# Inverting 16x16 instead of 32x32 blocks on VectorE in the first four rounds, with one more doubling on TensorE

## The chip, the cores and the metric

One core of one Trainium2 chip. The metric is the device time of one execution in microseconds (us). Engines: PE is TensorE, PEld its weight load, DVE is VectorE, ACT is ScalarE, POOL is GpSimd, SP is SyncE, which here only issues transfers (its queue is written SPq). In the timelines below VectorE, ScalarE and SyncE work through their instructions in the order in which the program gave them: what stands first in such a queue and waits holds up all that stands behind it (10.89 us at VectorE's `x`, in the profile after).

## The reference, cut to what matters

```python
for t in range(S):                                  # S = 768 steps, batch 4, 8 heads of width 40
    y[:, :, t] = einsum('bhd,bhde->bhe', rt, state)
    Sa = einsum('bhde,bhe->bhd', state, at)
    state = state * wt[:, :, None, :] - einsum('bhd,bhe->bhde', Sa, bt) + einsum('bhd,bhe->bhde', vt, kt)
x = y.transpose(0, 2, 1, 3).reshape(3072, 320)
h = x @ w_in                                        # 320 -> 1024
e = exp(h - max(h)); solu = h * e / (sum(e) + 1e-9)
ln = (solu - mean) / sqrt(var + 1e-6) * g_ln
return ln @ w_out                                   # 1024 -> 320
```

The kernel does the recurrence in 12 rounds of 64 steps. Within a round the term with `Sa` couples each step to the earlier ones; that is a triangular system, so every round needs the inverse of a unit triangular 64x64 matrix per batch and head.

## The kernel before

A round is two iterations of the main loop (even: batches 0 and 1, odd: 2 and 3), 24 in all. The parts that the argument touches, with cuts marked by `...`:

```python
def gather(n):                      # 64 blocks of 32x32, from DRAM, where scatter put them
    nb = of_round[n]["nb"] = two.tile([P, Q, Q], FP32, tag="blk", name="blk", bufs=2)
    for p in range(2):
        nc.sync.dma_start(out=nb[half(p)], in_=of_round[n]["blocks"])

def invert(n):                      # 30 steps, two VectorE operations each
    ...
    for j in range(1, Q - 1):
        ...
        nc.vector.tensor_tensor(out=t, in0=nb[...], in1=u[...], op=ALU.mult)
        nc.vector.tensor_tensor(out=u[...], in0=u[...], in1=t, op=ALU.subtract)
        yield
    nc.vector.tensor_copy(out=ut, in_=u.rearrange("p c t -> p t c"))
    ...                             # stores u and ut to DRAM; bring_inverse fetches them

def solve(i):                       # one doubling: from 32x32 inverses to a 64x64 inverse
    for q, t in zip((0, 2), products("py", [left(0), left(2)])):
        nc.scalar.copy(out=y_mid[quarter(q + 1)], in_=t)
    yield
    for q, z in zip((0, 2), products("pz", [right(0), right(2)])):
        nc.scalar.mul(out=tinvT[quarter(q), :, :, quarter(1)], in_=z, mul=-1.0)
    yield

def readout(i):
    ...
    if s == 0:                      # one buffer: waits until the last round's repack has read it
        of_round[n]["x"] = two.tile([P, G, 2, P], FP32, tag="x", name="x", bufs=1)
    nc.vector.tensor_tensor(out=of_round[n]["x"][...], in0=t[...], in1=d["exT"][...], op=ALU.mult)

def repack(n):                      # x to xT, the layout that the MoE part reads: 12 transfers
    ...
EARLY = ("r r a W I r f W r r I W y r W a f L a I W s a f W a f I W s I f a W f", ...)
for i in range(N):
    ...                             # MoE work starts in iteration 6
    turns(EARLY[len(js) - 1] if i < LAG else STEADY, dict(I=inverse_steps(i)), **parts)
```

`turns` tells one step of each part per letter, and that is the order in every engine's queue: `r` recurrence, `y` readout, `I` inverse steps of the next round (as many as `inverse_steps` says at each place), `s` solve for the next iteration, `a`, `f`, `g` the products that prepare later iterations, `L` loads, `W` narrowing of the MoE weights from 64-bit floats (fetch on SP, arithmetic on DVE and ACT).

## Time and profile before

| | before |
|---|---|
| time, median of 3 runs at first | 722.13 us |
| first `pu` (end of the start-up) | 64.0 us |
| iterations 0 to 6, from `pu` to `pu` | 25.3, 29.2, 26.4, 25.1, 27.3, 25.1, 25.8 us |
| later iterations while the MoE part runs beside them | 24.3 us (24.30 and 24.38 in turn) |
| PE, DVE, ACT, POOL busy | 84, 65, 38, 11% |

`pu` is the product that applies the finished inverse, once an iteration. I took its start from TensorE's timeline, so a list of iteration lengths is one profiled execution each, good to about 1 us. First, TensorE's longest waits in iterations 1 to 5 of the kernel before (columns: who waits and for whom, then us in total, number of times, longest):

```profile
PE pbT L267 <- ACT tinvT L505: 18.7, 5, 5.9
PE pcx L347 <- ACT y_mid L502: 9.9, 5, 5.3
```

Then VectorE's waits in the same stretch. VectorE waits twice, in the even iterations 2 and 4, for the transfers that still read `x`, and three times, in the odd ones, for the gathered blocks:

```profile
DVE x L602 <- DMA xT<-x: 11.6, 2, 6.7
DVE u L410 <- DMA blk<-blk_dram: 9.9, 3, 4.7
```

### The profile page before, as it was taken

The numbers are of one execution on the slowest core, as the hardware profiler recorded it, in microseconds if no ns is written. First come the engines' busy times: TensorE is split into PE (matmuls) and PEld (weight loads), VectorE is DVE, ScalarE is ACT, GpSimd is POOL, SyncE is SP. The second block draws the span as 40 slices with busy tenths as digits, with TensorE's granted clock in tenths as the row PEclk, the third lists the DMA queues.
The fourth block names the chain that finished last, engine by engine and source line by source line (L and its number), as shares of the span: only waits on it lengthen the run. The fifth ranks groups of instructions, "written<-read, shape, count | busy, mean of one in ns | idle before, by whom it ended". The sixth has DMA issues, their size and how long they took to land.

```text
span 719.9 us, 25430 instructions
## 1 busy us (share of the span) xinstructions
PE 606.7 (84%) x10873; PEld 428.9 (60%) x10873; DVE 468.7 (65%) x1310; ACT 275.1 (38%) x654; POOL 77.7 (11%) x128
## 2 busy tenths in 40 slices
PE   4524866767658899999999999999999899979997
PEld 3423655556546666667766666666666666545554
DVE  2387969658656959687687596786876754232442
ACT  3322534343343534443454345344533344312322
POOL 3202010010010111011100110111000000000000
PEclk9856975786797999999999999999999999998999
DMA  9964553743765353545554626545325131000001
GB/s 175 163 114 81 122 108 77 142 97 72 141 108 93 67 99 70 110 85 91 100 96 90 105 57 108 102 88 103 65 49 103 27 64 33 21 23 18 19 7 30
DMA packets 269791, 59.82 MB, mean 83 GB/s; under 512 B 255464, under 2 KB 265328, under 8 KB 269680
## 3 DMA queue, kind: packets, MB, share of 16 engines
q1 hardware_dynamic: 266416, 57.48, 42.8%
q8 instruction: 86, 1.41, 0.9%
q10 hardware_dynamic: 3264, 0.72, 0.7%
q14 instruction: 25, 0.20, 0.1%
HBM read 40.08 MB, written 13.37 MB: 74 GB/s over the span
## 4 chain that ended last, share of the span: by engine, by line
PE 54%; DVE 21%; DMA 8%; ACT 7%; issue 5%; SPq 5%; ACTq 0%; DVEq 0%
PE po L668 15%; PE h L623 10%; DVE u L422 6%; DVE prod L420 5%; PE pyo L595 4%; PE plnT L663 4%; PE pcx L347 3%; PE pcum L334 2%; DVE nmax L633 2%; DMA ut_dram<-ut 2%; PE ppsi L286 2%; DMA blk<-blk_dram 2%; PE plamu L286 2%; PE pyo L517 2%; PE plamv L286 2%
## 5 line engine op out<-in xcount | busy, mean ns | idle before, releaser
L623 PE MATMUL h<-w_in,xT 128*128 128x512 f32 (+1 forms) x288 | 128.2, 635 | 3.9 <-DVE e L640 3.9
L668 PE MATMUL po<-w,lnT 128*128 128x320 f32 x384 | 114.8, 438 | 0.0
L422 DVE TENSOR_TENSOR u<-u,prod 128x30 f32<-128x30 f32 (+4 forms) x360 | 96.5, 268 | 12.3
L420 DVE TENSOR_TENSOR prod<-blk,u 128x30 f32<-128x30 f32 (+4 forms) x360 | 93.5, 260 | 11.5 <-DMA blk<-blk_dram 1.0
L668 PEld LDWEIGHTS po<-w,lnT 128*128 128x128 f32 x384 | 69.0, 190 | 26.2 <-issue 2.9
L337 POOL TENSOR_TENSOR kx<-raw_b,inv 128x320 f32<-128x320 f32 x24 | 21.0, 877 | 351.3 <-ACT inv L335 308.0
L633 DVE TENSOR_REDUCE nmax<-h 128x1 f32<-128x1024 f32 x24 | 29.3, 1221 | 44.9 <-PE h L623 44.9
L623 PEld LDWEIGHTS h<-w_in,xT 128*128 128x128 f32 (+1 forms) x288 | 38.2, 191 | 31.7 <-issue 29.8
L602 DVE TENSOR_TENSOR x<-pyo,kx 128x512 f32<-128x512 f32 x24 | 16.6, 692 | 60.8 <-PE pyo L595 49.1
L673 ACT ACTIVATE osb<-po,rs 128x320 f32<-128x320 f32 x24 | 12.7, 527 | 96.9 <-PE po L668 76.3
L347 PE MATMUL pcx<-cst,lw 128*128 128x132 f32 x192 | 34.3, 311 | 10.3 <-ACT y_mid L502 9.9
L347 PEld LDWEIGHTS pcx<-cst,lw 128*128 128x128 f32 x192 | 29.8, 214 | 19.4 <-ACT y_mid L502 15.2
L664 ACT COPY lnT<-plnT 128x512 f32<-128x512 f32 x48 | 28.0, 594 | 33.2 <-PE plnT L663 33.2
L637 ACT ACTIVATE e<-h,nmax 128x1024 f32<-128x1024 f32 x24 | 26.7, 1114 | 36.2 <-DVE nmax L633 36.2
L267 PE MATMUL pbT<-cst,kx 128*128 128x128 f32 x96 | 17.9, 321 | 25.8 <-ACT tinvT L505 18.7
L640 DVE TENSOR_TENSOR e<-h,e 128x1024 f32<-128x1024 f32 x24 | 29.4, 1225 | 14.8 <-ACT e L637 14.3
L334 PE MATMUL pcum<-lw,cst 128*128 128x320 f32 x48 | 23.2, 572 | 18.4 <-ACT lw L330 9.0
L663 PE MATMUL plnT<-cst,e 128*128 128x128 f32 x192 | 31.4, 294 | 6.2 <-DVE e L640 5.4
L288 DVE TENSOR_TENSOR lamv<-plamv,cst 128x512 f32<-128x512 f32 x24 | 16.5, 689 | 27.3 <-PE plamv L286 27.2
L505 ACT ACTIVATE tinvT<-pz 32x256 f32<-32x256 f32 x48 | 17.8, 372 | 42.5 <-PE pz L490 42.0
L267 PEld LDWEIGHTS pbT<-cst,kx 128*128 128x128 f32 x96 | 12.3, 163 | 35.4 <-issue 35.4
L663 PEld LDWEIGHTS plnT<-cst,e 128*128 128x128 f32 x192 | 22.1, 147 | 18.3 <-ACT kT L269 6.6
(104 smaller groups left out, 1087.8 us busy)
## 6 DMA issues: line engine op xcount, KB each, us to landing
blk<-blk_dram SPq DMA_DIRECT2D x24, 256.0 KB
raw_k<-in_k_dram SPq DMA_DIRECT2D x24, 160.0 KB
v<-in_v_dram SPq DMA_DIRECT2D x24, 160.0 KB
r<-in_r_dram SPq DMA_DIRECT2D x24, 160.0 KB
out_dram<-osb SPq DMA_DIRECT2D x24, 160.0 KB
raw_w<-in_w_dram SPq DMA_DIRECT2D x23, 160.0 KB
raw_b<-in_b_dram SPq DMA_DIRECT2D x23, 160.0 KB
raw_a<-in_a_dram SPq DMA_DIRECT2D x23, 160.0 KB
```

Source lines behind the costliest of these rows:

```text
L267: nc.tensor.transpose(out=t[:, g * P:(g + 1) * P], in_=pair(src, g), identity=ident)
L286: nc.tensor.matmul(t[half(c ^ p * cross), p, g * L:(g + 1) * L], lhsT=lhs[half(p), g, half(c)], rhs=rhs[half(p), g, half(c)], start=True, ...
L334: nc.tensor.matmul(t[:, 0:DM], lhsT=c_("cum_in"), rhs=lw[:, :, 0:D], start=True, stop=True)
L347: nc.tensor.matmul(t[:, g * 132:g * 132 + 132], lhsT=pair(lw, 2 * j + g), rhs=cst[:, lo:lo + 132], start=True, stop=True)
L420: nc.vector.tensor_tensor(out=t, in0=nb[:, j:j + 1, j + 1:Q].to_broadcast([P, rows, m]), in1=u[:, 0:rows, j:j + 1].to_broadcast([P, rows, ...
L422: nc.vector.tensor_tensor(out=u[:, 0:rows, j + 1:Q], in0=u[:, 0:rows, j + 1:Q], in1=t, op=ALU.subtract)
L595: nc.tensor.matmul(t[half(p), c, g * W:g * W + used], lhsT=kb[half(c), j, 2 * g + p, :], rhs=lam[half(c), h % 2, h // 2, 0:used], start=i ...
L623: nc.tensor.matmul(h[:, j * 512:j * 512 + 512], lhsT=of_round[i // 2]["xT"][rows, kt, i % 2 * P:i % 2 * P + P], rhs=w_in[rows, 4 if kt == ...
L633: nc.vector.tensor_reduce(out=nmax, in_=h, axis=AX.X, op=ALU.max, negate=True)
L640: nc.vector.tensor_tensor(out=q, in0=h, in1=e, op=ALU.mult)
L663: nc.tensor.transpose(out=t[:, j * P:(j + 1) * P], in_=q[:, f * P:(f + 1) * P], identity=ident)
L668: nc.tensor.matmul(o[:, 0:DM], lhsT=lnT[:, f, :], rhs=w2[:, f, :], start=f == 0, stop=f == NF - 1)
```

## The change

The intent: VectorE's inversion is on the path of the start-up and of the early iterations, so give it half the rows (28 short operations instead of 60) in rounds 0 to 3 and let TensorE, which waits there, do the doubling from 16 to 32 by products. Two copies go from ACT to POOL, the first loads are reordered, and six products whose result nobody reads are put ahead of the first chains. The diff, cut to its core (`...` marks cuts):

```diff
+FINE = 4
...
-        nc.scalar.copy(out=keyed(a)[:, :, :, 0:D], in_=by_heads(given(i, "a")))
+        nc.gpsimd.tensor_copy(out=keyed(a)[:, :, :, 0:D], in_=by_heads(given(i, "a")))
...
+    def invert_fine(n):
+        ...
+        for j in range(1, R - 1):                       # R = 16
+            ...                                         # the same two VectorE operations
+        for key, t, src in (("ut", ut, x.rearrange("b c t -> b t c")), ("u", u, x)):
+            for z in range(2):
+                nc.scalar.copy(out=t[half(z)][:, :, R * z:R * z + R], in_=src[half(z)])
+            for z in range(2):
+                nc.sync.dma_start(out=dst[:, R * z:R * z + R, :], in_=t[half(z)])
...
-        nc.scalar.copy(out=lamv[:, :, :, L:], in_=...)
+        nc.gpsimd.tensor_copy(out=lamv[:, :, :, L:], in_=...)
...                                                      # in solve:
+        if fine:
+            t = products("py16", [... for q in range(4)])
+            nc.scalar.copy(out=y_mid, in_=t[:, 0])
+            yield
+            t = products("pz16", [... for q in range(4)], [... for q in (0, 2)])
+            for q in (0, 2):
+                nc.vector.scalar_tensor_tensor(out=x, in0=t[quarter(q), 1, :, :, 0:R], scalar=c_("low")[quarter(q)],
+                                               in1=x, op0=ALU.mult, op1=ALU.add)
+            for q in range(4):
+                nc.scalar.mul(out=tinvT[rows, :, :, c:c + R], in_=t[rows, 0, :, :, R:Q], mul=-1.0)
+            yield
...
-    EARLY = ("r r a W I r f W r r I W y r W a f L a I W s a f W a f I W s I f a W f", ...
+    EARLY = ("r r a W I r f W r r I W y r W a s f L a W I s W a f a W s I f a W s I f W f", ...
...                                                      # inverse_steps, iterations 1 to 4
-            return [0, 0, 6, 6, 5 if i < LAG - 1 else 2] if i % 2 else [4, 4, 4, 3, 0]
+            return [0, 0, 2, 3, 3] if i % 2 else [3, 3, 2, 0, 0]
...                                                      # before the loop
-        load(0, "k", "v")
+        load(0, "k")
+        warm(3, sm_t[0].rearrange("q c g d -> q (c g d)"))
...                                                      # v and r later, weights behind round 0's gather
+        warm(3, of_round[0]["spilt"])
```

In what follows "sums" are the two VectorE operations after `pz16` and "scalings" the four ScalarE ones.

## The prediction

> **What bounds the kernel now.** I read four views in this order: the page's busy totals and slices, a table of four stretches, the chain of waits inside one early round, and TensorE's own waits in the late part. One round is two iterations of the main loop (0 to 23), one inversion and one block of each input. Iteration i is told by its `pu` product. The timeline has `pu` at 63.99, 89.32, 118.47, 144.84, 169.94, 197.23 and 222.32 us (iterations 0 to 6) and about every 24.4 us after that.
>
> ```profile
> PE   4524866767658899999999999999999899979997
> PEclk9856975786797999999999999999999999998999
> 0.00:64.00 64.00, 27.75 (x378) 22.08 (x378) 33.65 (x115) 18.40 (x43) 10.36 (x23) 0.75 0.84 141
> 64.00:222.30 158.30, 108.52 (x2483) 88.68 (x2482) 115.05 (x377) 65.18 (x173) 16.54 (x24) 0.78 0.54 105
> 222.30:640.00 417.70, 399.47 (x7769) 278.19 (x7770) 290.06 (x763) 171.81 (x404) 47.00 (x74) 0.99 0.42 78
> ```
>
> The columns of the last three lines are PE, PEld, DVE, ACT, POOL, then granted clock, DMA share and GB/s. From 222 us on PE is busy 96% of the time at clock 0.99: there PE is the bound. Before that it is busy 43% and 69% at clock 0.75 and 0.78, and DVE is the busiest engine (73% in the second stretch). So the kernel has three parts: a start-up of 64 us, six early iterations of 158 us (26.4 each), and a part limited by PE. The change can win only where PE waits.
>
> The start-up is one series of waits; the chain's lines around round 0's inversion:
>
> ```profile
> 31.90 0.66 DVE u L410
> 52.71 0.61 DVE ut L426
> 54.01 3.32 DMA u_dram<-u
> ```
>
> The blocks are not in SBUF before 31.8 us although their gather is issued at 23.6. DVE then takes 20.8 us, and the first product that uses the inverse starts at 59.0. DMA is busy 84% of this stretch.
>
> In the early iterations the chain goes through DVE in the odd iteration and through SP's queue in the even one:
>
> ```profile
> 150.71 4.33 DMA blk<-blk_dram
> 155.06 0.42 DVE u L410
> ...
> 161.34 1.08 PE pbT L267 x4
> ...
> 165.80 0.36 SPq L442
> ...
> 181.55 2.66 DMA xT<-x
> ...
> 184.53 0.69 DVE x L602
> ...
> 186.06 4.87 DMA bits<-in_moe_w_out_dram
> ...
> 191.23 0.43 ACT parts L167
> ```
>
> Here DVE is held until the gather lands (155.06), works through inversion steps mixed with weight pieces, and releases ACT and PE late. SP cannot start to fetch the inverse (165.8) before DVE has freed a landing buffer of the weights. From there SP issues about 26 transfers, one after the other, until 186.1, and DVE waits for the weight piece behind them until 190.96. `pu` of iteration 5 follows 6.3 us later.
>
> **What the Trainium skill says.** "VectorE: DVE Perf Modes", Rules for kernel authors, advises for chained operations to keep their number small, since each pays its own pipeline drain. The trace agrees: a step on 15 elements takes 0.18 us and one on 128 elements 0.29, so most of a step is fixed. "TensorE: Matmul & The Clock Gate", Part 1, says that the array runs at half clock until it has been busy for a window of about 3.4 us. The trace agrees in size: two `pcum` products take 1.43 us at 6.46 and 0.70 at 19.64. "GPSIMD Engine Reference", 4.1 Engine selection, puts two-input operations at about twice VectorE's time and one-input ones near its rate. The first half agrees (128x320 with two inputs: 0.88 us on POOL, 0.48 on DVE); no run has shown a copy on POOL yet. "DMA: Bandwidth & Descriptors", Anatomy of one DMA, gives a fixed cost of about 2 us that is mostly the write's receipt, for the software queue. These are hardware queues, and the trace shows more (3.32 us above, 128 KB), so the number of round trips counts and this change keeps it at two (scatter and gather, store and fetch).
>
> **The change, part by part.**
>
> ```profile
> L422 DVE TENSOR_TENSOR u<-u,prod 128x30 f32<-128x30 f32 (+4 forms) x360 | 96.5, 268 | 12.3
> L420 DVE TENSOR_TENSOR prod<-blk,u 128x30 f32<-128x30 f32 (+4 forms) x360 | 93.5, 260 | 11.5 <-DMA blk<-blk_dram 1.0
> ```
>
> *DVE.* One inversion of 32x32 blocks has 60 of these: (96.5 + 93.5) / 12 = 15.8 us, plus 0.02 to 0.04 between two of them (1.8 together), plus scale, clears and transposed copy (0.53 + 0.49 + 0.22 + 0.61 = 1.9): 19.5 us. With 16x16 blocks it has 28, on 14 to 56 elements, which take 0.18 to 0.22: 5.7, plus gaps 0.8, plus scale and clear 0.5: 7.0 us. The first doubling adds two DVE operations per iteration, estimated at 0.3 each from the 128-element steps, so 1.2 per round. Net: 11.3 us of DVE less in each of rounds 0 to 3. Rounds 4 to 11 keep the old form.
>
> *PE and ACT.* The first doubling adds 32 + 32 + 16 = 80 products of 32x32 in each of 8 iterations. Such a group of 32 takes 0.63 to 0.75 us, so 1.6 to 1.9 us per iteration. ACT gets one more copy (0.4) and four small multiplications (0.3 each), 1.6 per iteration, and loses the copies of `a` (0.45) and into `lamv` (0.46): 0.7 more. Per round four half copies of the inverse (0.4 each) come on top.
>
> *Start-up.* Four weight transfers (three of 256 KB and the row of g) move behind round 0's gather, and v and r behind more urgent loads. What stands ahead of the gather falls from about 3.9 to 3.1 MB. Without `a` in ACT's queue, the second front no longer waits behind raw_a (landed at 9.5). I expect scatter at about 17 us (20.0 before) and the gather landed at 25 (31.8). DVE then needs 7.0 + 3.3 for `lamv`, two `kx` and two `nt` between the steps, about 36 with a stall; copies 1.5; store and fetch 6 (7.0 before, from the end of DVE to the first product), about 43.5; then four product steps instead of two. The old two took 5.0 us (59.0 to 64.0), the new ones about 7.5. First `pu` at 51: **13 us won**. The unread products are in idle PE time; they warm the clock for the first 10 us of products (a part of the 3 us above) and for the doublings.
>
> *Early iterations.* Iteration 0 is full of DVE (18.4 of 20 us between 60 and 80): 20 steps of about 0.6 become 8 of 0.45, so 8 less of which I count 6. In iterations 1 and 3, 17 steps become 8: 9.9 - 3.8 = 6.1 us on the chain shown above. Iterations 2 and 4 hang on SP, whose count of transfers does not fall: 1 each. Iteration 5 keeps 14 steps of the coarse round 4: 1. Sum 6 + 6 + 6 + 1 + 1 + 1 = 21; the longer solve and ACT's extra work take back about 0.5 per iteration: **18 us won**.
>
> *Late part.*
>
> ```profile
> PE pcum L334 <- ACT sT L548: 5.5, 12, 0.7
> PE pnt L286 <- ACT x_own L474: 3.4, 6, 0.6
> ```
>
> These are PE's longest waits between 240 and 560 us. PE's idle time there is 11.5 us in all. ACT's copy of `a` stands just ahead of `sT` (370.71 to 371.06), so moving it brings `sT` 0.4 us sooner and removes most of the first line: **5 us won**. POOL is 11% busy and takes two more copies of roughly 0.5 us per iteration; that is hidden.
>
> Sum: 722 - 13 - 18 - 5 = 686; I say **685 us**.
>
> **Rivals.** (1) SP's queue becomes the bound of all early iterations. It speaks for it that SP is on the chain for 16 us of a 52 us round, that `x` waited 11.6 us for `xT`, and that no transfer is dropped; against it, that about 34 us of issuing per round leaves 18 free. Then an odd iteration gains 3, not 6, and the time is about 697. (2) The four-step solve takes the place of the inversion: PE, ACT and DVE hand over eight times, and in the start-up nothing lies beside it. If it takes 11 us instead of 7.5 and delays `pu` by 1.5 in each iteration, the time is about 697. (3) PE was waiting for DVE in more places than I count, so the early iterations fall to what PE needs: 108.5 us in six iterations, some 18 each at clock 0.78, 20 with the new products. That wins 38 instead of 18: 665. Its clock would rise too. (4) POOL's copies delay the `sm` product that carries the state, as POOL works in order: `sm` takes 0.72 us and waits 55 us for `tot`, so there is room; about 0.5 us per iteration at worst, 697.
>
> **Range and chances.** The start-up's gain is the surest (9 to 17), the early one the widest (8 to 38), the late one small (0 to 8). Together 17 to 63, and the ends are unlikely to come together: 668 to 702. Below 707.7 is faster by over 2%, which needs 14 us, about what the start-up alone gives: 0.94. Within 2%: 0.05. Slower: 0.01.
>
> **What would show it.** PE has 10,873 + 640 + 6 products, DVE 1310 - 124 instructions; the fine DVE steps are 0.18 to 0.22 us each. The gather lands at about 25 us and the first `pu` stands at 51 (wrong if over 56). `pu` to `pu` falls to about 20 in iterations 0, 1 and 3 and stays within 2 us in 2, 4 and 5; if all six fall alike, rival 3 holds and my reading of SP is wrong; if SP's queue has no gaps, rival 1. From iteration 6 on the spacing should be 24.0 instead of 24.4, with the wait of `pcum` for `sT` nearly gone; an unchanged spacing means that ACT did not matter there.

## More of the kernel before

`products` takes its accumulator from a pool of two PSUM banks, which the prefix sums `pcx` and most transposes use as well.

## The result, and the profile after

The changed kernel took 740.59 us (739.54 to 746.65, four runs), the kernel before beside it 721.07. The ratio is 1.029, with an interval of 1.022 to 1.037. It is slower. Ratios here and below are the mean time of one kernel's runs over that of the other's runs in the same rounds, so they are not quite the ratio of the medians that I quote. Executions over 1.5% slower than the fastest of the same kernel are left out of the means.

The changed kernel's page and its three stages, against the lines that the prediction shows (first the busy totals, then the stages with PE, PEld, DVE, ACT, POOL, clock, DMA share and GB/s):

```profile
PE 633.8 (86%) x12165; PEld 451.7 (61%) x12165; DVE 432.0 (59%) x1186; ACT 279.3 (38%) x662; POOL 102.0 (14%) x192
```

```profile
0.00:64.00 64.00, 39.80 (x581) 28.16 (x582) 25.02 (x86) 20.11 (x46) 15.82 (x39) 0.75 0.83 136
64.00:222.30 158.30, 112.69 (x3195) 92.98 (x3195) 77.43 (x244) 69.13 (x186) 24.09 (x44) 0.75 0.48 94
222.30:640.00 417.70, 393.94 (x7810) 280.30 (x7809) 292.85 (x789) 163.69 (x381) 57.68 (x102) 0.97 0.43 80
```

VectorE's instructions came out as counted (1186), and its busy time over the whole run fell by 36.7 us (468.7 to 432.0), where four times 11.3 had been predicted. (The second stage shows 37.6 us less, but it is cut at the same times in both kernels, and the changed one is behind there.) TensorE's count did not come out: 12,165 and not 10,873 + 640 + 6. The trace shows each of these fp32 products as two records, so the prediction's "group of 32" was 16 products. The 80 new ones take 2.0 us in iterations 3 and 5 all the same, close to its 1.6 to 1.9, because 32 of them (64 records) take 0.75 us, as long as 16 took before. That is luck.

Yet the time rose, and the clock of the second stage is 0.75 instead of 0.78. The lengths say where:

| | first `pu` | i0 | i1 | i2 | i3 | i4 | i5 | i6 | `pu` 7 to the end |
|---|---|---|---|---|---|---|---|---|---|
| before | 64.0 | 25.3 | 29.2 | 26.4 | 25.1 | 27.3 | 25.1 | 25.8 | 471.8 |
| after | 62.6 | 27.5 | 29.1 | 35.0 | 24.1 | 34.5 | 27.0 | 34.7 | 463.3 |

The start-up won 1.4 us instead of 13; three iterations lost 7 to 9 us each; the late part won 8.5. The waits of iterations 1 to 5 in the changed kernel name the two even ones:

```profile
PE pcx L351 <- ACT tinvT L565: 26.8, 5, 10.2
DVE x L678 <- DMA xT<-x: 21.9, 2, 11.0
ACT ut L441 <- DVE u L435: 21.5, 2, 11.0
```

The kernel before had 9.9, 11.6 and no such line. The timelines of iteration 2 show how the three hang together. Each line is start, duration, engine, operation; the bracket is the idle time before it and what ended it. SyncE's queue, VectorE, ScalarE and TensorE of the changed kernel in turn:

```profile
121.33 2.05 SPq L316 DMA_DIRECT2D r<-in_r_dram  x2
123.42 3.19 SPq L689 DMA_DIRECT2D xT<-x  x3
...
132.69 1.19 SPq L692 DMA_DIRECT2D xT<-x  x2
```

```profile
124.12 0.23 DVE L168 TENSOR_SCALAR parts<-bits 128x160 int32<-128x160 int32 x1
135.24 0.69 DVE L678 TENSOR_TENSOR x<-pyo,kx 128x512 f32<-128x512 f32 x1 [10.89 <-DMA xT<-x]
...
138.66 0.18 DVE L435 TENSOR_TENSOR u<-u,prod 128x14 f32<-128x14 f32 x1
138.75 0.69 DVE L561 SCALAR_TENSOR_TENSOR tinv<-pz,cst,tinv 32x128 f32<-32x128 f32 x2
```

```profile
128.01 0.39 ACT L353 ACTIVATE kx<-pcx 128x264 f32<-128x264 f32 x1 [0.27 <-PE pcx L351]
138.88 1.27 ACT L441 COPY ut<-u 64x256 f32<-64x256 f32 x2 [10.48 <-DVE u L435]
...
141.02 1.14 ACT L565 ACTIVATE tinvT<-pz 16x128 f32<-16x128 f32 x4
```

```profile
131.36 0.66 PE L271 MATMUL prT<-cst,r 128*128 128x128 f32 x4
142.22 1.25 PE L351 MATMUL pcx<-cst,lw 128*128 128x132 f32 x4 [10.21 <-ACT tinvT L565]
```

SyncE issues the twelve transfers of the repack from 123.42 to 133.88, so `x` cannot be overwritten before 135.24. Behind `x` in VectorE's queue stand the last inverse step and the sums; ScalarE's next instructions are the copies of that inverse and then the scalings; TensorE's next is `pcx`, which needs the bank that the scalings and the sums read. One late transfer stops all three, and TensorE comes back 7.0 us after `x` and cold: `pcx` takes 1.25 us for two products (four records), and took 0.72 at 127.20.

In iteration 6 the same sums stand behind the coarse inversion of round 4 and the scaling of the MoE weights (VectorE, then ScalarE):

```profile
257.88 1.01 DVE L253 SCALAR_TENSOR_TENSOR w<-w,g_col,mean 128x320 f32<-128x320 f32 x2
258.81 0.68 DVE L292 TENSOR_TENSOR psi<-ppsi,cst 128x512 f32<-128x512 f32 x1
259.41 0.69 DVE L561 SCALAR_TENSOR_TENSOR tinv<-pz,cst,tinv 32x128 f32<-32x128 f32 x2
```

```profile
260.18 1.15 ACT L565 ACTIVATE tinvT<-pz 16x128 f32<-16x128 f32 x4 [5.88 <-DVE tinv L561]
```

The scalings wait for the sums although neither needs the other's result. They read the same PSUM bank, and in six of the eight first doublings of this run they start 0.08 us after the sums have ended. The Trainium skill's "PSUM — Partial Sum Buffer", section "PSUM bank collisions raise a hardware error", says that two engines on one bank and the same 32 partitions must be kept apart, reads against reads included. The trace agrees as far as order goes: in none of the eight did the scalings start before the sums had ended.

In the late part, the wait at which the prediction aimed went as foreseen, from 5.5 us in 12 to

```profile
PE pcum L338 <- ACT sT L624: 1.6, 6, 0.3
```

and an iteration takes 23.75 us there instead of 24.3.

The first theory (T1) was therefore: the single buffer of `x` and what is queued behind it. Rivals: the additional products themselves (R1), and SyncE's queue as the bound (T-SP, the prediction's rival 1).

### The profile page after: what moved, and what is told of

It is laid out like the page before. It is cut to its first block, busy times and chain, and to the rows that moved or that the text cites.

```text
span 737.8 us, 27981 instructions
## 1 busy us (share of the span) xinstructions
PE 633.8 (86%) x12165; PEld 451.7 (61%) x12165; DVE 432.0 (59%) x1186; ACT 279.3 (38%) x662; POOL 102.0 (14%) x192
## 4 chain that ended last, share of the span: by engine, by line
PE 61%; DVE 12%; ACT 6%; SPq 6%; issue 4%; DMA 3%; DVEq 0%; ACTq 0%
PE po L744 13%; PE h L699 12%; PE pyo L671 4%; PE plnT L739 3%; PE pcx L351 3%; DVE prod L465 3%; PE pz L539 2%; DVE u L467 2%; PE py L539 2%; PE plamv L290 2%; DVE nmax L709 2%; PE pcum L338 2%; DMA blk<-blk_dram 2%; PE ppsi L290 2%; PE pyo L593 2%
## 5 line engine op out<-in xcount | busy, mean ns | idle before, releaser
L744 PEld LDWEIGHTS po<-w,lnT 128*128 128x128 f32 x384 | 69.5, 192 | 26.4 <-issue 3.3
L467 DVE TENSOR_TENSOR u<-u,prod 128x30 f32<-128x30 f32 (+7 forms) x240 | 65.1, 271 | 8.2
L465 DVE TENSOR_TENSOR prod<-blk,u 128x30 f32<-128x30 f32 (+7 forms) x240 | 65.5, 273 | 7.1
L749 ACT ACTIVATE osb<-po,rs 128x320 f32<-128x320 f32 x24 | 12.6, 527 | 97.2 <-PE po L744 86.4
L740 ACT COPY lnT<-plnT 128x512 f32<-128x512 f32 x48 | 27.5, 586 | 33.6 <-PE plnT L739 33.5
L713 ACT ACTIVATE e<-h,nmax 128x1024 f32<-128x1024 f32 x24 | 26.7, 1114 | 34.4 <-DVE nmax L709 34.4
L539 PE MATMUL py<-tinv,nt 32*32 32x32 f32 x1280 | 28.4, 204 | 9.1 <-DMA tinv<-ut_dram 7.4
L731 POOL TENSOR_TENSOR rs<-c,mhalf 128x1 f32<-128x1 f32 x24 | 13.2, 548 | 157.2 <-DVE c L730 157.2
L739 PE MATMUL plnT<-cst,e 128*128 128x128 f32 x192 | 29.5, 282 | 5.7 <-DVE e L716 5.4
L581 ACT ACTIVATE tinvT<-pz 32x256 f32<-32x256 f32 x48 | 17.9, 373 | 43.5 <-PE pz L539 43.2
L657 POOL TENSOR_TENSOR sm<-tot,fac 128x320 f32<-128x320 f32 x20 | 14.9, 745 | 126.3 <-DVE tot L656 109.0
L539 PEld LDWEIGHTS py<-tinv,nt 32*32 32x32 f32 x1280 | 23.6, 115 | 14.3 <-DMA tinv<-ut_dram 9.0
```

Of the source, the lines that this page charges most:

```text
L465: nc.vector.tensor_tensor(out=t, in0=nb[:, j:j + 1, j + 1:Q].to_broadcast([P, rows, m]), in1=u[:, 0:rows, j:j + 1].to_broadcast([P, rows, ...
L467: nc.vector.tensor_tensor(out=u[:, 0:rows, j + 1:Q], in0=u[:, 0:rows, j + 1:Q], in1=t, op=ALU.subtract)
L539: nc.tensor.matmul(t[quarter(out), c:c + Q], lhsT=lhs(p, g), rhs=rhs(p, g), start=True, stop=True)
L739: nc.tensor.transpose(out=t[:, j * P:(j + 1) * P], in_=q[:, f * P:(f + 1) * P], identity=ident)
L740: nc.scalar.copy(out=lnT[:, fs.start:fs.stop].rearrange("p f t -> p (f t)"), in_=t)
L744: nc.tensor.matmul(o[:, 0:DM], lhsT=lnT[:, f, :], rhs=w2[:, f, :], start=f == 0, stop=f == NF - 1)
```

## The experiments

All 16 passed the comparison with the reference, also the four that leave arithmetic out. So passing shows little about small errors here. The kernels of one round of experiments share a chip and the runs of the kernel before (medians 721.3, 722.4, 720.6 and 720.2 us in the four rounds).

### First round: the buffer of x, the place of the last inverse steps, the copies

**Two buffers for x in the changed kernel.** To make room the gathered blocks got one buffer instead of two. The order of all engines stayed the same.

```diff
-    of_round[n]["x"] = two.tile([P, G, 2, P], FP32, tag="x", name="x", bufs=1)
+    of_round[n]["x"] = two.tile([P, G, 2, P], FP32, tag="x", name="x", bufs=2)
-    ... tag="blk", name="blk", bufs=2)
+    ... tag="blk", name="blk", bufs=1)
```

> The changed kernel with two buffers instead of one for the readout's tile x (and one instead of two for the gathered blocks, to make room); every engine's order of instructions stays. Theory T1 (in iterations 2 and 4 the readout on VectorE waits 11 us for the DMAs that still read x, and the last inverse steps, the sums into the fine inverse and, through them, ScalarE and TensorE wait behind it): the wait of x for the DMA falls from 21.9 us in two to under 2, iterations 2 and 4 shrink from 35.0 and 34.5 us to 26 to 29, iteration 6 (34.7) stays, and the time falls from 740.6 by 12 to 17 us, to 724 to 728. Rival R1 (the four-step solve and its 80 more products an iteration are themselves the cost): the wait goes, but iterations 2 and 4 stay above 32 us and the time above 736.

731.4 us, ratio 1.015. Iterations 0 to 6: 27.6, 28.7, 27.1, 27.8, 28.4, 27.0, 35.0. The wait is gone and iterations 2 and 4 fell as expected, but iteration 3 rose from 24.1 to 27.8: some of the stall had been caught up there. Net 10.6 us over iterations 0 to 5, under the 12 expected, and the time missed the expected 724 to 728. T1 is right about the wait, but it explains by the medians only 9 of the 20 us lost: all of iterations 1 to 5 now take 27 to 28.7 us, and the kernel before needs 24.9 to 29.1 with the same buffers.

**The same in the kernel before (control).**

> The control: the kernel before with the same two buffers for x. There the same wait is 11.6 us in two places, but DVE had inversion work queued ahead of it, and iterations 2 and 4 were 26.4 and 27.3 us against 25 for their odd neighbours. T1: the wait goes and iterations 2 and 4 come down by 1 to 2 us each: 717 to 719 us. If the wait alone, without the queue behind it, cost what it lasts, it would be 710.

721.6 us, ratio 1.001: no gain. Iterations 2 and 4 came down by 1.5 and 1.1 us as expected, but my edit cost 2.6 us at the start: with a single block buffer the gather of round 1 had to wait for the inversion of round 0. In the control SyncE issues it at 53.07, in the kernel before at 50.03. The wait of 11.6 us was worth 2.3 in iterations 1 to 5; I put that down to the inverse work that VectorE had to do in front of it.

**All inverse steps and copies ahead of x.**

```diff
-            return [0, 0, 2, 3, 3] if i % 2 else [3, 3, 2, 0, 0]
+            return [0, 0, 2, 3, 3] if i % 2 else [4, 4, 0, 0, 0]
```

> The changed kernel with the inverse steps of iterations 2 and 4 told as 4 and 4 instead of 3, 3 and 2, so that the last steps and the four ScalarE copies of the inverse stand ahead of the readout x instead of behind it. T1 with the queue reading: ScalarE is free when x ends, only the bank of the fine products is still tied to the sums behind x; the restart after x takes 3 to 4 us instead of 7, iterations 2 and 4 lose about 3 us each, time 733 to 736. If the wait of x alone holds the recurrence and not what is queued behind it, nothing changes (740).

735.8 us, ratio 1.020; iterations 2 and 4 took 32.0 and 32.7. As expected: what is queued behind the wait counts besides the wait.

**The kernel before with only the two copies on POOL.**

```diff
-        nc.scalar.copy(out=keyed(a)..., in_=...)
+        nc.gpsimd.tensor_copy(out=keyed(a)..., in_=...)
-        nc.scalar.copy(out=lamv..., in_=...)
+        nc.gpsimd.tensor_copy(out=lamv..., in_=...)
```

> The kernel before with only the two copies (a, and v into lamv) moved from ScalarE to GpSimd. If this part is what shortened the late iterations of the changed kernel (24.4 to 23.75 us, 7 us in sixteen), this kernel gains that and a little early: 711 to 714 us. If the late gain came from something else in the change, it stays at 719 to 721.

711.96 us, ratio 0.987. The stretch from `pu` 7 to `pu` 23 takes 371.4 us; it took 379.8 before and 372.8 in the changed kernel. The whole late gain of the change, and a little more, is this part alone.

### Second round: is VectorE's inversion the bound, and what does the doubling cost

**Half of the inversion left out of the kernel before** (wrong), with one and with two buffers for x.

```diff
         for j in range(1, Q - 1):
+            if j % 2 == 0:
+                yield
+                continue
```

> The kernel before with every second step of the 32x32 inversion left out (a wrong result on purpose): VectorE loses about as much work per early iteration (some 3.5 us) as the change takes from it, and nothing else changes. If VectorE's inversion bounds the early iterations, as the prediction's second step says, iterations 1 to 5 (29.2, 26.4, 25.1, 27.3, 25.1 us) lose about 3 us each and the time goes to 702 to 708 us (some of it at the start-up). If they are held by something else (T1: the transfers behind x and the order of TensorE's work), VectorE only reaches x earlier and waits there longer: iterations 2 to 5 within 1 us of before, time 712 to 719, all of it from the start-up and iteration 0.

> The same half inversion, with two buffers for x, so that the wait of x for its DMAs is out of the way too (wrong result on purpose). If VectorE was a bound hidden behind that wait, iterations 2 to 5 fall from 24.9, 25.4, 26.2, 25.2 to 22 to 23 us; if TensorE's string of products with its waits and its lowered clock is the bound, they stay at 24 to 25 us.

695.7 and 693.5 us, ratios 0.962 and 0.959.

| | first `pu` | i0 | i1 | i2 | i3 | i4 | i5 | i6 |
|---|---|---|---|---|---|---|---|---|
| before | 64.0 | 25.3 | 29.2 | 26.4 | 25.1 | 27.3 | 25.1 | 25.8 |
| half inversion | 61.7 | 19.0 | 24.8 | 29.8 | 21.1 | 29.6 | 20.8 | 24.1 |
| half inversion, two x | 61.9 | 18.1 | 23.9 | 29.1 | 20.8 | 27.7 | 22.5 | 24.2 |

Both expectations missed, in an instructive way. About 9 of the 26 us lie after `pu` 7 (371.1 us from `pu` 7 to `pu` 23, against 379.8), since rounds 4 to 11 are halved as well: there the wait of `pcum` for `sT` fell from 5.5 to 2.4 us with the copies still on ScalarE. VectorE's inversion is a bound in the iterations 0, 1, 3 and 5: they lost 4 to 6 us, near what the prediction gave to 0, 1 and 3. But 2 and 4 grew by 3.5 and 2.3 us. They did so with two buffers too (29.1 and 27.7, against 24.9 and 26.2 in the control), so the wait on x was not the last thing there. In that kernel VectorE and TensorE stop in iteration 2 at

```profile
125.98 0.24 DVE L162 TENSOR_SCALAR parts<-bits 128x160 int32<-128x160 int32 x1 [11.64 <-DMA bits<-in_moe_w_out_dram]
...
127.66 1.09 PE L267 MATMUL pbT<-cst,kx 128*128 128x128 f32 x4 [12.06 <-ACT tinvT L508]
```

that is, at the next piece of MoE weights, whose fetch had stood behind the repack and two loads in SyncE's queue:

```profile
117.92 1.19 SPq L619 DMA_DIRECT2D xT<-x  x2
...
122.41 1.30 SPq L211 DMA_DIRECT2D bits<-in_moe_w_out_dram  x2
```

From 101 to 129 us this queue has hardly a gap: it issues for 25.7 of the 28.0 us. In the kernel before, adding up single entries, SyncE issues for 24.0 of the 26.4 us of iteration 2 and 24.8 of the 27.3 of iteration 4 (91%), but only 12.1 of the 25.1 of iteration 3. The pairs 2 + 3 and 4 + 5 have 36.1 of 51.5 and 47.8 of 52.4 us; in the changed kernel it is 39.4 of 59.0 and 50.4 of 61.6. The prediction's 34 of 52 fits the first pair and not the second. (The 43 to 53 us in an expectation below came from merged lines of the timeline, which count the gaps between transfers as issuing.) T-SP came up from here.

**The changed kernel with two x and without the first doubling** (no `py16`, `pz16`, copy, sums and scalings; wrong).

> The changed kernel with two buffers for x and without the first doubling (no products py16 and pz16, no copy, sums and scalings after them; a wrong result on purpose); the order of the rest stays. If the 80 products and the two more hand-overs an iteration are what is left of the loss (27.1, 27.8, 28.4, 27.0 us against 24.9 to 26.2 of the kernel before with the same buffers), iterations 2 to 5 fall to 24 to 25.5 us, and iteration 6, where the fine solve waits behind the coarse inversion, from 35.0 to 25 to 27; time 731 to about 708 to 712. If the order of the other work is to blame, iterations 2 to 5 stay above 26.5 us and iteration 6 above 31.

694.5 us, ratio 0.962. First `pu` at 56.9, then 25.1, 22.7, 28.8, 20.6, 29.7, 19.5, 26.3. The total fell much further than expected (708 to 712). So what the kernel with two x still loses is this doubling: 4.4 us in the start-up, 20.3 in iterations 0 to 5, 8.7 in iteration 6. What is left has the same pattern as the half inversion, with VectorE waiting 7.1 and 8.5 us in the two even iterations for weight pieces behind SyncE's queue, which the expectation had not allowed for.

**A candidate: fine inversion in round 0 only,** two x, and the stores of the first inverse ahead of the second round's loads.

```diff
-FINE = 4
+FINE = 1                       # EARLY, inverse_steps as in the kernel before, solve steps kept
...
         scatter(1)
-        load(2, "b", "k")
-        gather(1)
         turns("I a", dict(I=99), a=at, I=inv)
         warm(3, of_round[0]["spilt"])
+        gather(1)
         bring_inverse(0)
+        load(2, "b", "k")
```

> A candidate to beat both: fine inversion for the first round only, the later rounds as in the kernel before; the copies on GpSimd and the load order of the changed kernel; two buffers for x; and the stores of the first inverse issued ahead of the second round's loads on the DMA queue. The start-up reading (stores ready at 41.1 us but issued at 45.9 because the queue's order put a scatter, two loads and a gather ahead): the first pu moves from 61.3 to 56 to 58 us. Iterations 1 to 6 as in the kernel before with copies on GpSimd (711 us, first pu 63.1): 704 to 707 us. If the start-up is bound elsewhere (weights on VectorE, the four-step solve), the first pu stays at 60 to 62 and the time at 709 to 711.

719.0 us, ratio 0.995. SyncE's queue in the changed kernel, and then in this one:

```profile
38.25 2.44 SPq L399 DMA_DIRECT2D blk_dram<-nt  x4
40.79 1.32 SPq L316 DMA_DIRECT2D raw_b<-in_b_dram  x2
42.20 1.76 SPq L316 DMA_DIRECT2D raw_k<-in_k_dram  x2
44.13 1.62 SPq L409 DMA_DIRECT2D blk<-blk_dram  x2
45.85 1.42 SPq L443 DMA_DIRECT2D ut_dram<-ut  x2
```

```profile
37.88 2.25 SPq L399 DMA_DIRECT2D blk_dram<-nt  x4
40.24 1.16 SPq L443 DMA_DIRECT2D ut_dram<-ut  x2
```

The stores went out 5.6 us sooner and the first `pu` came at 58.5, just above the expected 56 to 58 (2.9 sooner than with two x, 4.1 sooner than in the changed kernel). But iteration 0 took 33.6 us and iteration 1 30.2. Probably the weights that had been put off in the start-up, the fine doubling and the full inversion meet there: VectorE is busy for 27.0 us of iteration 0, against 15.5 with two x. The clock is lower too (0.71 against 0.81), and no run separates the two. The candidate failed.

### Third round: SyncE's queue, the bank, and the repairs together

**Weight fetches on ScalarE's queue, in the changed kernel** (one x).

```diff
-                nc.sync.dma_start(out=to[row:row + part.shape[0]], in_=part)
+                nc.scalar.dma_start(out=to[row:row + part.shape[0]], in_=part)
...
         for j, (dst, _) in enumerate(pieces):
+            if j:
+                fetch(j + 2)
...
-            fetch(j + 3)
```

> The changed kernel with the fetches of the MoE weights issued by ScalarE's queue instead of SyncE's (16.2 us of the 52.6 us that SyncE spent issuing between the pu products of iterations 2 and 4); one buffer for x as before. Theory T-SP (in the early iterations SyncE issues transfers one after another for 43 to 53 us of each pair's 50 to 61, and xT, which x waits for, lands late because of it): the wait of x for xT falls from 11 to 3 to 7 us in iterations 2 and 4, time 728 to 735. Rival (the transfers themselves or the scalar queue limit): the wait stays, ScalarE is disturbed, time 740 or more.

727.5 us; the ratio is 1.008. The profile fell into the one slow run of the four (739.8 us, clock 0.859), so I use only its order of events: the repack's transfers start 7.7 us before `pu` of iteration 2 (115.66 and 123.39) instead of 4.2 us after it (123.42 and 119.21), and no wait of x for `xT` is left in iterations 1 to 5. I had expected 3 to 7 us to remain. The bytes moved are the same. Two things left SyncE's queue. One is the issuing of the fetches: by single entries only 4.0 and 2.3 us in the two pairs of the changed kernel, not the expectation's 16.2, which counts gaps. The other is what the fetches waited for, a landing buffer that VectorE has to free; all behind them in the queue waited too. In iterations 2 and 3 of the changed kernel these were SyncE's longest waits:

```profile
SPq L215 <- DVE w L178: 7.5, 3, 4.3
SPq L215 <- DVE parts L176: 5.2, 1, 5.2
```

"DMA: Bandwidth & Descriptors", section "Issuing engines are not separate DMA queues", says that issuing on several engines only saves issue time, "usually small relative to the DMA itself". The issue time of these fetches was small here (0.3 to 1.4 us each), and yet this one edit won 13 us of median. So most of the gain is probably the waiting that left the queue; no run separates it from the issuing.

**The same in the kernel before with the copies on POOL.**

> The kernel before with the two copies on GpSimd and the weight fetches on ScalarE's queue: a candidate. T-SP: the pairs of iterations 2+3 and 4+5 (52.1 and 52.0 us with the copies alone) come down by 1 to 3 us each, down to what VectorE's inversion needs, and the time from 712 to 706 to 710. Rival: VectorE's inversion bounds those pairs anyway, or the fetches hold ScalarE up: 711 to 715.

705.5 us, ratio 0.978, just better than expected. Iterations 2 and 3 together fell from 52.2 to 48.9 us, 4 and 5 from 52.0 to 45.5. (In the kernel with the copies alone the fetches' issuing took 5.4 and 3.4 us of these pairs, and their waits at the head of the queue over 13 and 2.) Now VectorE's wait for the gathered blocks stands out (iterations 1 to 5):

```profile
DVE u L411 <- DMA blk<-blk_dram: 15.5, 3, 5.8
```

**A bank of its own for the first doubling** (changed kernel, two x; the hidden layer's accumulators are free until iteration 6).

```diff
-            t = bank(name)
+            t = ps2.tile([P, DFF], FP32, tag="h", name=name)[:, 0:512] if early else bank(name)
```

> The changed kernel with two buffers for x, and the products of the first doubling in the first iterations in the accumulators of the hidden layer (unused until iteration 6) instead of one of the two banks that pcx also needs. Leaving the doubling out took 33 us off the early part. If hand-over through the bank is the larger share of that, TensorE's wait at pcx (12.6 us in five) goes and iterations 1 to 5 lose 2 to 3 us each: 716 to 721 us against 731 with two buffers alone. If the products and their place in TensorE's order are the share, pcx only waits less and the time stays at 727 to 731.

727.5 us, ratio 1.009 against 1.015. The wait at `pcx` (12.6 us in five) went and this came:

```profile
PE plamv L290 <- ACT rT L273: 15.0, 5, 4.4
```

The copy of `rT` stands behind the scalings in ScalarE's queue. The bank was a way on which the wait travelled, not its cause; by its number the run spoke for the second reading, by its trace for neither.

**The repairs together** (fine inversion for three rounds, two x, own bank, stores first, fetches on ScalarE).

> All that the runs suggest for the changed kernel together: fine inversion for three rounds (not in iteration 6, whose 35 us would become 25 to 27), two buffers for x, the hidden layer's accumulators for the first doubling, the stores of the first inverse ahead of the second round's loads, weight fetches on ScalarE's queue. The sum of the single effects from 740.6: 10 for x, 9 for iteration 6, 3 for the start-up, 5 to 10 for the bank, 2 to 4 for the queue: 703 to 712 us. If the parts lean on the same waits: 712 to 720.

712.6 us, ratio 0.987: the edge between the two expectations. Single repairs did not add up, and their kernel was no better than the kernel before with two copies moved.

### Fourth round: products or hand-over

Open was whether TensorE's 80 products an iteration or the sums and scalings after them cost the 33 us.

**All products, but no sums and scalings** (changed kernel, two x; wrong).

```diff
-            for q in (0, 2):
-                ...  nc.vector.scalar_tensor_tensor(...)
-            for q in range(4):
-                ...  nc.scalar.mul(...)
             yield
```

> The changed kernel with two buffers for x, all products of the first doubling and the copy between them, but without VectorE's sums and ScalarE's scalings after the second set (a wrong result on purpose). If the hand-over through VectorE's queue is the cost, nearly all of the 33 us between it and the kernel without the doubling goes: the odd iterations 3 and 5 fall from 27.8 and 27.0 to 21 to 23.5 us, iteration 6 from 35.0 to 26 to 28, time 699 to 709. If the products themselves are the cost, the iterations stay above 26, iteration 6 above 31, and the time above 718.

704.4 us, ratio 0.979. First `pu` 60.2, then 26.1, 22.8, 29.1, 22.6, 28.7, 21.6, 27.6. Of the 36.9 us between the medians of the kernels with and without the doubling (731.4 and 694.5), the products cost 9.9 and the hand-over 27.0. Here "hand-over" is the sums and scalings with all that waits for them: their own work is gone too. The next run keeps that work and changes only the order.

**All work, but the steps that wait for the blocks later** (changed kernel, two x).

```diff
-            return [0, 0, 4, 5, 5]
+            return [0, 0, 0, 7, 7]
-            return [0, 0, 2, 3, 3] if i % 2 else [3, 3, 2, 0, 0]
+            return [0, 0, 0, 4, 4] if i % 2 else [3, 3, 2, 0, 0]
```

> The changed kernel with two buffers for x and all its work; the first inverse steps of the next round, which wait for the gathered blocks, moved from the third place of an odd iteration to the fourth and fifth, so that the sums of the doubling stand ahead of them in VectorE's queue. Hand-over reading: iterations 1, 3 and 5 fall from 28.7, 27.8, 27.0 by 2 to 4 us each; iteration 6 stays at 35; time from 731 to 720 to 725. If the products are the cost, nothing changes: 729 to 733.

721.8 us, ratio 1.002 against 1.015. This is iteration 3 with two x before that edit, VectorE, ScalarE and TensorE:

```profile
157.12 0.29 DVE L423 TENSOR_SCALAR u<-blk 128x256 f32<-128x256 f32 x1 [2.06 <-DMA blk<-blk_dram]
...
157.75 0.71 DVE L561 SCALAR_TENSOR_TENSOR tinv<-pz,cst,tinv 32x128 f32<-32x128 f32 x2
```

```profile
158.54 1.15 ACT L565 ACTIVATE tinvT<-pz 16x128 f32<-16x128 f32 x4 [4.67 <-issue]
```

```profile
154.87 0.65 PE L271 MATMUL prT<-cst,r 128*128 128x128 f32 x4
159.74 1.25 PE L351 MATMUL pcx<-cst,lw 128*128 128x132 f32 x4 [4.21 <-ACT tinvT L565]
```

The sums stand behind an inverse step that waits for a gather. With that step moved, the sums of iteration 3 ran 10.4 us after its `pu` (155.71) instead of 13.0, iterations 1 to 5 took 22.3, 30.2, 25.1, 27.9 and 25.0 us (the odd ones 2.0 to 6.5 less, iteration 2 3 more), and 8.5 us were won in them. By the medians the order alone is worth 9.6 of the 27.0 us of the hand-over. Iteration 0 of this execution took 32.3 us against 27.6, with the same products in the same order. Its stage line and that of the kernel without the edit differ in the clock, 0.61 against 0.81:

```profile
60.60:92.90 32.30, 27.19 (x567) 22.57 (x566) 15.25 (x44) 14.98 (x38) 4.40 (x7) 0.61 0.45 93
```

```profile
61.30:88.90 27.60, 20.93 (x565) 17.10 (x564) 15.49 (x43) 14.88 (x38) 4.59 (x7) 0.81 0.54 108
```

So a single iteration can differ by some 5 us from run to run by the clock alone.

**The changed kernel repaired.** As the repaired kernel above, with the two product sets in two banks, the scalings told ahead of the sums (in its trace they start 1.9 us before the sums end), and the later steps.

> The changed kernel repaired: fine inversion for three rounds, two buffers for x, the two sets of products of the first doubling in two banks of the hidden layer's accumulators, the scalings ahead of the sums so that ScalarE does not wait for VectorE, the later inverse steps moved behind the gathered blocks, stores of the first inverse ahead of the second round's loads, weight fetches on ScalarE's queue. Its forerunner took 712.6. If the hand-over is the cost: 698 to 705. If the products are: 708 to 713.

707.5 us (699.9 to 711.4, so the spread is wide), ratio 0.979. A miss: above the 698 to 705 of the hand-over reading, and just under the 708 to 713 of the other. Its profiled run counts as slow (1.6% above its fastest), so I read no iteration from it. What holds it is open; the products, worth 9.9 us above, remain in it in any case.

**The best: the kernel before, copies on POOL, fetches on ScalarE, later inverse steps.**

```diff
-            return [0, 0, 6, 6, 5 if i < LAG - 1 else 2] if i % 2 else [4, 4, 4, 3, 0]
+            return [0, 0, 0, 9, 8 if i < LAG - 1 else 5] if i % 2 else [4, 4, 4, 3, 0]
```

> The kernel before with the two copies on GpSimd, the weight fetches on ScalarE's queue (705.5), and the inverse steps of the odd iterations, of which the first waited 5.4 to 5.8 us for the gathered blocks, moved from the third place to the fourth and fifth. If that wait of VectorE's whole queue is on the path, iterations 1, 3 and 5 (29.4, 28.7, 26.0) lose 2 to 4 us each: 696 to 701. If VectorE's amount of work bounds them, nothing changes: 703 to 707.

699.5 us (697.8 to 701.9), ratio 0.972. Iterations 1 to 5: 27.5, 21.3, 25.4, 18.6, 26.7, that is 4.3 us less than its forerunner. The wait of 15.5 us for the blocks is gone from VectorE's list; its longest is now

```profile
DVE lamv L289 <- PE plamv L287: 7.7, 3, 3.6
```

Iterations 1 and 3 fell by 1.8 and 3.3 us, iteration 5 did not. This kernel beats both, and it has nothing of the fine inversion in it.

## Why the prediction was wrong, point by point

The 17.9 us between the two profiled executions, added up from the runs (differences of the lengths above). Each entry rests on one execution and is good to a few microseconds: that of the kernel with two x is 4 us faster than its median, that without the doubling 2 us slower.

| part | us | from |
|---|---|---|
| start-up without the doubling | -7.1 | no doubling (56.9) less before (64.0) |
| less inversion and all else but the doubling, with two x, iterations 0 to 5 | -12.0 | no doubling (146.4) less before (158.3) |
| the same, iteration 6 | +0.5 | 26.3 less 25.8 |
| doubling in the start-up | +4.4 | two x (61.3) less no doubling (56.9) |
| doubling in iterations 0 to 5 | +20.3 | 166.7 less 146.4 |
| doubling in iteration 6 | +8.7 | 35.0 less 26.3 |
| single buffer of x behind it | +11.6 | after less two x: 1.3, 10.6, -0.3 |
| from `pu` 7 on | -8.5 | after (463.3) less before (471.8) |

**The step that failed** is one term of the early iterations: "the longer solve and ACT's extra work take back about 0.5 per iteration". It was 3.4 us on average in iterations 0 to 5 and 8.7 in iteration 6, for which nothing had been entered; with the single buffer of x behind it, 10.6 us more. The average hides where it lies: 2.5 us in iteration 0, 6.0, 7.2 and 7.6 in the odd ones, and -1.7 and -1.3 in 2 and 4, which without the doubling are held by SyncE's queue anyway. I had counted the products' durations (1.6 to 1.9 us) and taken them for filling of idle time. For the products that was right by more than half: with a duration of about 2.0 us each time they lengthened the six iterations by 4.5 us together. What I had not asked is in whose queue the doubling's hand-over stands: the sums are VectorE's, and VectorE's queue holds a wait for a transfer in every early iteration of the changed kernel (x in the even, the blocks or weight pieces in the odd ones). Before, only ScalarE stood between the two product groups of the solve. The hand-over cost 15.9 us in iterations 0 to 5 (166.7 less 150.8) and 7.4 in iteration 6.

**Less VectorE work.** Right for iterations 0 and 1 in kind, and for 3 as well: the half inversion took 6.3, 4.4 and 4.0 us from them, where 6 each were entered. Wrong for 5, which gave 4.3 and not 1, and wrong in sign for 2 and 4: they were entered with 1 each and gave back 3.5 and 2.3, since SyncE's queue sets the pace of the even iterations. Of the 21 us entered, 12 to 13 came.

**The start-up.** The gather landed at 25.96 (25 predicted). The inverse was ready at 39.0 instead of 36, its copies took 2.1 instead of 1.5, store and fetch 9.9 instead of 6 (of that 4.7 us in SyncE's queue behind a scatter, two loads and a gather, from 41.14 to 45.85), and from the first product to `pu` 11.6 instead of 7.5. That is 11.6 us lost of 13. The reordered queue confirms the middle term in part: stores 5.6 us sooner brought `pu` 2.9 us sooner than with two x. The unread products did not warm the clock for the doublings: they ran from 41.3 to 46.1, TensorE then waited 4.9 us for the fetch, and from 51 to 64 us the granted clock was 0.50 in both kernels.

**The late part.** Mechanism right, size small: 5 predicted; the two copies alone gave 8.4 between `pu` 7 and `pu` 23. The wait that the prediction named accounts for 3.9 of them (5.5 to 1.6 us); the rest is not traced. POOL took the copies without harm, on which the prediction had no run: 128x320 took 0.52 and 0.45 us in the mean there, and 0.45 and 0.46 on ScalarE. "GPSIMD Engine Reference" (4.1, Engine selection) calls one-input operations on POOL roughly line-rate; the runs agree as far as ScalarE goes, and none has the same copy on VectorE.

**The rivals.** Rival 1 (SyncE's queue) held in the even iterations and for x, shown by the fetches moved to another queue, though as much by what the queue waits for as by what it issues. Rival 2 (the solve takes the place) is what happened, but I had sized it at 1.5 us an iteration and stopped at 697: with both at once, and with the wait for x in front, the sum passes zero. I had treated the rivals as alternatives, while one queue's wait lengthened the other's. The chance of 0.01 for slower was too small for that.

**The marks named in advance** worked: the first `pu` came at 62.6 ("wrong if over 56"), `pu` to `pu` of about 20 in 0, 1 and 3 did not show, 2 and 4 moved by far more than 2 us, and SyncE issued for 27.1 of the 35.0 us of iteration 2 and 26.0 of the 34.5 of iteration 4, with the gaps only at their end.

Open: why the repaired changed kernel stays 2 us above the slowest that its parts promised (705), what share of the 20.3 us is the lower clock after each stop rather than the stop, and how the gain of the moved fetches divides between issuing and waiting.

## What to carry to other kernels

Before moving work from a loaded engine to an idle one, look at which in-order queues the new hand-overs pass through, and whether any of them holds a wait for a transfer ahead of the new instruction; there a step of 0.7 us can cost several. Take a wait away at its root (a second buffer, another issuing queue, a later place) before making the engine that waits faster, since a faster engine only reaches the wait sooner. And read a transfer queue like an engine's: add up its issue time per loop pass (91% of the even iterations here, although each transfer is short), entry by entry and not from merged lines, and look for transfers in it that wait for a buffer (12.7 us in two iterations), since all behind them wait too.

## What the Trainium skill lacked or had wrong

- "DMA: Bandwidth & Descriptors" ("Issuing engines are not separate DMA queues") calls issue time usually small relative to the DMA. For one transfer it was: an entry of SyncE's queue took 0.3 to 1.9 us in iterations 2 to 5 of the changed kernel (median 0.6). The sum was not: 10.5 us for the twelve small ones of a repack (123.42 to 133.88), and 24.0 of the 26.4 us of iteration 2 in the kernel before. Nor does the section say that a transfer which waits for its buffer holds up those behind it in the issuing queue: 12.7 us in iterations 2 and 3 of the changed kernel. Moving such transfers to ScalarE's queue took the median from 740.6 to 727.5 us.
- "TensorE: Matmul & The Clock Gate" (Part 1) has the clock rise after about 3.4 us of sustained work. In one execution TensorE worked from 79.98 to 92.89 us with hardly a gap on products of 32 to 128 rows at a granted clock of 0.50 to 0.52, and four transposes still took 0.98 us at the end (0.66 in another execution with the same products); the mean clock of the whole iteration was 0.61 against 0.81. What Part 1 warns of (idle gaps, a clock seen stuck at a quarter) does not cover this.
- "PSUM — Partial Sum Buffer" states that two readers of one bank must be kept apart, and the eight first doublings of the changed kernel keep to it. It does not say that the second reader thereby inherits the first one's queue: 5.9 us of waiting in iteration 6 for an operation whose result it does not use.
